# Pooled attention and a gated layer on one core: the denominators of 16 heads folded to 64 partitions, and the order searched

## The chip, the cores and the metric

The kernel runs on one core of a Trainium2 chip. The metric is the device time of one execution, in microseconds, as the median of several runs; less is better. Engine names are those of the profile: PE is the matrix engine (PEld its weight loads), DVE the vector engine, ACT the scalar engine, POOL the GpSimd engine, SP the queue that issues most transfers.

## What is computed

Attention with queries that are averaged in pairs, then a gated layer on its result. B = 4, H = 8, S = 1152, D = 64; d_model = 512, d_ff = 1536.

```python
q_pool = q.reshape(B, H, S // 2, 2, D).mean(axis=3)
scores = 1 / np.sqrt(D) * np.matmul(q_pool, k.transpose(0, 1, 3, 2))
scores = scores - np.max(scores, axis=-1, keepdims=True)
attn = np.exp(scores)
attn = attn / (np.sum(attn, axis=-1, keepdims=True) + 1e-09)
x = np.matmul(attn, v)          # then (B, H, S/2, D) -> (B * S/2, H * D)
gate = 1.0 / (1.0 + np.exp(-(x @ w_gate)))
out = (gate * (x @ w_val)) @ w_out
```

## The kernel before, in words

There are 32 heads, numbered u = 0 to 31, and each has 576 pooled queries in two halves of 288 columns (`GR`, `GN`). A half walks over 9 chunks of 128 keys (`NC`). To keep float32 accuracy, values are split into a high part in the type float32r and a low part that is what the high one left over, so that one product becomes two or three.

For one chunk of one half, `half` records: the scores, two products into a PSUM bank (L579); the exponential on ACT, once rounded to float32r into `eh` (L583) and once in full back into the bank (L612); the difference of the two on DVE into `el` (L615); the product of `eh` with the values into the bank `av[0]` (L622), and of `el` into `av[1]` (L626). Heads 0 to 7 (`WHOLE`) do it in plain float32 instead, with L597. Ahead of a head stand its maxima: 12 products of 384 columns (L473) and their reductions on DVE (L479).

The sum of the probabilities, the denominator, is built on POOL for heads 8 to 31. `acc` is [128, 2, 288]: POOL adds the `eh` tiles of two chunks at a time (L644), folds the two halves of `acc` into one (L651) and adds the ninth chunk (L654). Now every partition holds the sum over 9 keys, and what is left is a sum over 128 partitions. For that, ACT rounds `acc` to its high part (L692, `acc_hi`), POOL subtracts it to get the low part (L695, `acc_lo`), and PE multiplies each of the two [128, 288] tiles with a matrix of ones, `ones2`, into `av[1]` (L699, `den`). So the denominator takes two products for each half:

```python
for k in range(2):
    nc.tensor.matmul(out=tl(av[1])[:, 0:GN], lhsT=ones2, rhs=tl(dh)[:, k], start=False, stop=(k == 1))
```

After it DVE and ACT take the numerators and denominators out of the banks (L675 to L684), `normalise` divides, and splits the result into high and low parts `x` (L736, L740). The gated layer (`gated`, L815) of one batch element runs between the attention steps of the next one; the last one's runs alone at the end. Its operands `wg` and `wo` are loaded by SP, and its results pass DVE, ACT and POOL (L858, L864, L868, L872).

The order is not that of the code. `Plan` collects every step as an operation with an engine, an estimated duration, a priority and the buffers that it takes (`SLOTS` says how many there are of each: 4 `el`, 2 `t`, 2 `pp`, 1 `acc`, 2 `dh`, 8 banks `b`). `Plan.run` plays the plan through: each engine takes the ready operation with the lowest priority number, and the order that comes out is the order in which the instructions are emitted. Each engine then works through its own list in that order.

Of the kernel before, what the change touches and what calls it, by code (L numbers as in the profile page):

```python
# [37 lines left out]
class Plan:  # L38
# [16 lines left out]
    def op(self, eng, dur, fn, prio, after=(), uses=(), take=(), late=0.0, keep=0.0, behind=None):  # L55
# [7 lines left out]
        return o  # L63

    def run(self):
        n_dep = {}
        ready = {e: [] for e in self.LAT}
        for k, o in enumerate(self.ops):
            o.key = (o.prio, k)
            o.at = 0.0  # L70
            n_dep[o] = len(o.after)
            for a in o.after:
                a.users.append(o)
            if o.behind:
                n_dep[o] += 1
                o.behind.next.append(o)
# [3 lines left out]
        for t, hs in self.holds.items():  # L80
            for k, h in enumerate(hs):
                h.k = k
                left[h] = len(h.ops)
                for o in h.ops:
                    of.setdefault(o, []).append(h)
# [16 lines left out]
        while done < len(self.ops):  # L102
# [7 lines left out]
            while again:  # L110
                again = False
                for e in self.LAT:
# [34 lines left out]
                    for h in of.get(o, ()):  # L147
                        left[h] -= 1
                        h.end = max(getattr(h, "end", 0.0), av + o.keep)
                        if left[h] == 0:  # L150
                            free[h.tag].append((h.end, h.slot))
                            heapq.heappush(times, h.end)
# [10 lines left out]
def attention_glu_kernel(ctx: ExitStack, tc: tile.TileContext, qT, kT, vt_in, v, wg, wv, wo, out):  # L163
# [11 lines left out]
    SLOTS = {  # L175
# [20 lines left out]
    def tiles(tag, shape, dt, pool=const):  # L196
        n = LATE.get(tag, 0) or SECOND.get(tag, 0)
        return [None] * n + [pool.tile(shape, dt, name=f"{tag}{i}") for i in range(n, SLOTS[tag])]
# [8 lines left out]
    def change_first():  # L207
# [30 lines left out]
        "dh": tiles("dh", SHAPE["dh"], F32R),  # L238
        "t": tiles("t", SHAPE["t"], F32),
        "e": tiles("e", [128, GN], F32, first_p),  # L240
        "ve": tiles("ve", [128, NC, 2, D], F32, first_p),
# [27 lines left out]
    def pe64(n):  # L269
        return n / 595  # L270
# [12 lines left out]

    AHEAD = 50
    KEEP = 0.15
    LAST_GATE = 215
# [266 lines left out]
    def half(u, g, st, hd, stat, vdep, pair, tk):  # L553
# [13 lines left out]
        for c in range(NC):  # L567
# [22 lines left out]
            if whole:  # L590
# [8 lines left out]
                if c in RUNS:  # L599
                    last = pl.op("PE", 0.1 + len(wait) * pe64(GN), pv, pos + 1,  # L600
                                 after=deps + [vdep] + (in_turn if first else [last]),
                                 uses=[stat] + [h for _, h in wait] + ([] if first else av), take=av + tk if first else [])
                    if first:
                        in_turn[:] = [last]
                    wait, deps = [], []
# [82 lines left out]
        if mine_c:  # L688
# [7 lines left out]

            def den():
                for k in range(2):
                    nc.tensor.matmul(out=tl(av[1])[:, 0:GN], lhsT=ones2, rhs=tl(dh)[:, k], start=False, stop=(k == 1))  # L699

            o = pl.op("ACT", act(GN), acc_hi, at, after=added, uses=[acc], take=[dh])
            o = pl.op("POOL", 0.85, acc_lo, at, after=[o], uses=[acc, dh])
            last = pl.op("PE", 2 * pe(GN), den, at + 2, after=[o, last], uses=[dh, av[1]])
        st["yo"][g].append(pl.op("DVE", 0.46, plus2, at + 1, after=[part, last], uses=[av[1], y]))
# [251 lines left out]
    for k in range(SLOTS["Q"]):  # L956
        for t in TL["Q"][k]:
            nc.vector.memset(t[:, SQ:SQ + 64].bitcast(F32), 0.0)
    order = pl.run()
    with tc.manual_schedule():  # L960
# [36 lines left out]
```

## Time and profile before

| | |
|---|---|
| median of 3 runs | 922.13 us (921.84 to 923.32) |
| the profiled execution | 923.2 us, of which the span from first to last instruction is 921.4 us |
| instructions | 18477, of them 6299 matrix products |
| busy share | PE 98%, PEld 95%, POOL 73%, ACT 72%, DVE 70% |
| HBM | 169 GB/s over the span |
| granted clock of PE | 0.998 of full speed |

A busy share is a mean over stages that differ: up to about 160 us the heads in plain float32, the conversion of the weights and most transfers; then attention and gated layer together; from 801 us on the last gated layer alone. A product that is recorded with 295 ns overlaps the next one, so the distance between two starts, not the recorded length, tells what a product costs where nothing waits.

### The profile page before, as it was taken

Reading aid. Unit: us, or ns where it says so; the run is one execution under the profiler, and the core shown is the slowest. Engines: PE = TensorE matmul, PEld = TensorE weight load, DVE = VectorE, ACT = ScalarE, POOL = GpSimd, SP = SyncE. Lnnn points to the kernel's source line nnn. Section 1 sums busy time; section 2 is a strip of 40 time slices with the busy share of each in tenths; the row PEclk is TensorE's granted clock in tenths of the full one; section 3 lists DMA queues with packets and bytes.
Section 4 is the critical chain, followed back from the end, with each engine's and each line's share of the span. In section 5 each row is a group of like instructions: output and inputs, shape, how many; then the busy total and the mean of one; then the engine's idle time right before and its main releaser. Section 6 shows DMA issues by size and latency. Waiting matters only on the chain.

```text
span 921.4 us, 18477 instructions
## 1 busy us (share of the span) xinstructions
PE 904.3 (98%) x6299; PEld 873.9 (95%) x6299; DVE 649.4 (70%) x1428; ACT 659.9 (72%) x1703; POOL 672.3 (73%) x668
## 2 busy tenths in 40 slices
PE   6999999999999999999999999999999999999998
PEld 5888888999999999999999999999999999999998
DVE  7778768888899888778687878877677874510112
ACT  4888888989998787677887677677877777322111
POOL 6755455989889899788989889888989877521211
PEclk9999999999999999999999999999999999999999
DMA  6999888789958566555544455544545423435432
GB/s 149 232 278 260 268 263 245 227 274 272 292 181 274 177 212 194 157 156 162 152 123 144 141 156 158 165 134 140 161 126 158 142 92 116 164 140 179 164 115 75
DMA packets 57614, 166.25 MB, mean 180 GB/s; under 512 B 17392, under 2 KB 21744, under 8 KB 51376
## 3 DMA queue, kind: packets, MB, share of 16 engines
q1 hardware_dynamic: 57360, 164.78, 58.7%
q8 instruction: 49, 0.80, 0.4%
q14 instruction: 45, 0.37, 0.1%
q10 hardware_dynamic: 160, 0.30, 0.1%
HBM read 132.12 MB, written 23.59 MB: 169 GB/s over the span
## 4 chain that ended last, share of the span: by engine, by line
PE 93%; DVE 3%; ACT 2%; DMA 1%; issue 0%; POOL 0%; SPq 0%; ACTq 0%; DVEq 0%; POOLq 0%
PE bank L815 48%; PE bank L579 16%; PE bank L473 8%; PE bank L597 7%; PE bank L626 6%; PE bank L622 6%; PE bank L699 1%; DMA wo<-wo_d 1%; DMA qr<-in_qT_dram 0%; DVE pm L479 0%; DVE pm L386 0%; DVE el L615 0%; ACT e L583 0%; POOL acc L654 0%; DVE pp L479 0%
## 5 line engine op out<-in xcount | busy, mean ns | idle before, releaser
L815 PE MATMUL bank<-x,wg 128*128 128x288 f32 x2304 | 356.0, 295 | 0.1
L815 PEld LDWEIGHTS bank<-x,wg 128*128 128x128 f32 x2304 | 327.0, 188 | 0.9 <-DVE pm L479 0.5
L615 DVE TENSOR_TENSOR el<-bank,eh 128x288 fp32r<-128x288 f32 x432 | 192.8, 452 | 69.8 <-ACT bank L612 65.3
L479 DVE TENSOR_REDUCE pm<-bank 128x1 f32<-128x384 f32 (+1 forms) x375 | 200.5, 551 | 52.6 <-PE bank L473 49.0
L583 ACT ACTIVATE eh<-bank 128x288 fp32r<-128x288 f32 x432 | 176.9, 409 | 73.7 <-PE bank L579 64.8
L579 PE MATMUL bank<-QA,KA 128*128 128x288 f32 x576 | 177.6, 311 | 2.5 <-DVE el L615 1.2
L612 ACT ACTIVATE bank<-bank 128x288 f32<-128x288 f32 x432 | 176.8, 409 | 0.1
L579 PE MATMUL bank<-QB,KB 128*128 128x288 f32 x576 | 169.0, 296 | 1.7 <-DVE QB L305 1.7
L872 POOL TENSOR_TENSOR g<-sg,g 128x288 fp32r<-128x288 f32 x96 | 80.2, 835 | 108.6 <-ACT g L868 106.7
L644 POOL TENSOR_TENSOR acc<-acc,eh 128x576 f32<-128x576 f32 x92 | 132.8, 1444 | 17.3 <-ACT eh L583 15.4
L815 PE MATMUL bank<-g,wo 128*128 128x288 f32 x864 | 139.2, 296 | 1.1 <-DMA wo<-wo_d 0.9
L473 PE MATMUL bank<-KA,QA 128*128 128x384 f32 (+1 forms) x375 | 126.9, 347 | 1.4 <-ACT e L583 0.7
L626 PE MATMUL bank<-el,vt 128*128 128x288 f32 x432 | 127.5, 295 | 0.0
L622 PE MATMUL bank<-eh,vt 128*128 128x288 f32 x432 | 127.4, 295 | 0.0
L815 PEld LDWEIGHTS bank<-g,wo 128*128 128x128 f32 x864 | 124.7, 188 | 2.1 <-DMA wo<-wo_d 1.1
L579 PEld LDWEIGHTS bank<-QA,KA 128*128 128x128 f32 x576 | 108.9, 189 | 9.0 <-DVE el L615 2.0
L579 PEld LDWEIGHTS bank<-QB,KB 128*128 128x128 f32 x576 | 109.1, 189 | 3.3 <-POOL qr L424 1.9
L864 DVE SCALAR_TENSOR_TENSOR sg<-sg,bank 128x288 f32<-128x288 f32 x96 | 43.2, 450 | 79.8 <-PE bank L815 77.9
L626 PEld LDWEIGHTS bank<-el,vt 128*128 128x128 f32 x432 | 81.1, 188 | 0.7 <-DVE y L678 0.3
L622 PEld LDWEIGHTS bank<-eh,vt 128*128 128x128 f32 x432 | 81.0, 188 | 0.5 <-ACT eh L583 0.2
L858 ACT ACTIVATE sg<-bank 128x288 f32<-128x288 f32 x96 | 39.4, 411 | 56.2 <-PE bank L815 54.0
L644 POOL TENSOR_TENSOR acc<-eh,eh 128x576 f32<-128x576 f32 x48 | 68.7, 1431 | 13.9 <-ACT eh L583 9.7
(83 smaller groups left out, 1380.4 us busy)
## 6 DMA issues: line engine op xcount, KB each, us to landing
wg<-wg_d SPq DMA_DIRECT2D x48, 1024.0 KB, 5.1
wo<-wo_d SPq DMA_DIRECT2D x36, 512.0 KB, 3.8
kr<-in_kT_dram SPq DMA_DIRECT2D x62, 288.0 KB, 5.2
wg_d<-cs SPq DMA_DIRECT2D x24, 512.0 KB, 5.3
qr<-in_qT_dram SPq DMA_DIRECT2D x31, 288.0 KB, 4.0
KP<-KA SPq DMA_DIRECT2D x30, 288.0 KB, 3.8
vr<-in_v_dram SPq DMA_DIRECT2D x24, 288.0 KB, 3.4
cr<-in_wg_dram SPq DMA_DIRECT2D x12, 512.0 KB, 5.9
```

What stands on the lines that cost most here:

```text
L473: nc.tensor.matmul(out=tl(m)[LO if t == 4 else ALL, 0:384], lhsT=lhs(t), rhs=rhs()[:, j * 384:(j + 1) * 384], start=True, stop=True)
L479: nc.vector.tensor_reduce(out=o, in_=tl(m)[p, 0:384], axis=AXX, op=ALU.max)
L579: nc.tensor.matmul(out=tl(m)[:, 0:GN], lhsT=tl(hd["k"])[k][:, ks], rhs=tl(hd["q"])[k][:, a:b], start=(k == 0), stop=(k == 1))
L583: nc.scalar.activation(out=ev(), in_=tl(m)[:, 0:GN], func=ACTF.Exp, scale=1.0 / 16.0)
L597: nc.tensor.matmul(out=tl(av[0])[:, 0:GN], lhsT=pair(c, 0), rhs=tl(h), start=(c == 0), stop=(c == NC - 1))
L612: nc.scalar.activation(out=p, in_=p, func=ACTF.Exp, scale=1.0 / 16.0)
L615: nc.vector.tensor_tensor(out=tl(el), in0=tl(m)[:, 0:GN], in1=ev().bitcast(F32), op=ALU.subtract)
L622: nc.tensor.matmul(out=tl(av[0])[:, 0:GN], lhsT=pair(c, w), rhs=ev(), start=(c == 0), stop=(c == NC - 1))
L626: nc.tensor.matmul(out=tl(av[1])[:, 0:GN], lhsT=pair(c, 1 - w), rhs=tl(el), start=(c == 0), stop=(c == NC - 1 and not mine_c))
L644: nc.gpsimd.tensor_tensor(out=tl(acc), in0=tl(old).bitcast(F32), in1=tl(eh).bitcast(F32), op=ALU.add)
L815: nc.tensor.matmul(out=ps[:, 0:GN], lhsT=l, rhs=r, start=(n == 0 and j == 0), stop=(n == 3 and j == 2))
L872: nc.gpsimd.tensor_tensor(out=g[:, 1, a:b], in0=tl(sg), in1=g[:, 0, a:b].bitcast(F32), op=ALU.subtract)
```

## The change

For heads 16 to 31 (`FOLD`) the sum over partitions is begun before PE. ACT copies the upper 64 partitions of `acc` into a new tile `ft` on partitions 0 to 63 (`down`, L745 of the changed kernel), and POOL adds it to the lower 64 (`fold2`, L749). The high part of this [64, 288] sum is written to the lower half of `dh[:, 0]` (`half_hi`, L736) and its low part to the upper half of the same tile (`half_lo`, L739), so that one product with ones over 128 partitions sums both (`den`, L730).

To make room, `el` has 3 buffers instead of 4, `t` and `pp` 1 instead of 2. The planner's estimate of the plain float32 product step (L597) loses its constant 0.1. And the order is taken from `search`: 30 times it draws a stretch of 30 us of the plan, shifts the priority of every operation in it (but those of SP) by up to 1 either way, plans anew, and keeps the shifts if the plan does not end later.

```diff
+    def search(self, rounds, width, shift):
+        dice = random.Random(1)
+        best = self.run()
+        end = max(o.end for o in best)
...
+        for _ in range(rounds):
+            at = dice.uniform(-width, end)
+            near = [(o, o.prio) for o, s, _ in made if at <= s <= at + width and o.eng != "SP"]
+            for o, p in near:
+                o.prio = p + dice.uniform(-shift, shift)
+            order = self.run()
+            new = max(o.end for o in order)
+            if new <= end:
+                best, end = order, new
...
+            else:
+                for o, p in near:
+                    o.prio = p
...
-        "b": 8, "K": 3, "Q": 3, "kr": 1, "qr": 1, "vr": 1, "vt0": 1, "vt1": 1, "eh": 4, "el": 4, "acc": 1, "dh": 2,
-        "t": 2, "pm": 2, "pp": 2, "KP": 1, "e": 6, "ve": 2,
+        "b": 8, "K": 3, "Q": 3, "kr": 1, "qr": 1, "vr": 1, "vt0": 1, "vt1": 1, "eh": 4, "el": 3, "acc": 1, "dh": 2, "ft": 1,
+        "t": 1, "pm": 2, "pp": 1, "KP": 1, "e": 6, "ve": 2,
...
+        "ft": tiles("ft", [64, GN], F32),
...
+    FOLD = lambda u: u >= 16
...
-                    last = pl.op("PE", 0.1 + len(wait) * pe64(GN), pv, pos + 1,
+                    last = pl.op("PE", len(wait) * pe64(GN), pv, pos + 1,
...
             def den():
+                if FOLD(u):
+                    nc.tensor.matmul(out=tl(av[1])[:, 0:GN], lhsT=ones2, rhs=tl(dh)[:, 0], start=False, stop=True)
+                    return
                 for k in range(2):
                     nc.tensor.matmul(out=tl(av[1])[:, 0:GN], lhsT=ones2, rhs=tl(dh)[:, k], start=False, stop=(k == 1))
 
+            def half_hi():
+                nc.scalar.activation(out=tl(dh)[LO, 0], in_=tl(acc)[LO, 0], func=ACTF.Copy)
+
+            def half_lo():
+                nc.gpsimd.tensor_tensor(out=tl(dh)[HI, 0], in0=tl(acc)[LO, 0], in1=tl(dh)[LO, 0].bitcast(F32), op=ALU.subtract)
+
+            if FOLD(u):
+                ft = pl.hold("ft")
+
+                def down():
+                    nc.scalar.activation(out=tl(ft), in_=tl(acc)[HI, 0], func=ACTF.Copy)
+
+                def fold2():
+                    o = tl(acc)[LO, 0]
+                    nc.gpsimd.tensor_tensor(out=o, in0=o, in1=tl(ft), op=ALU.add)
+
+                o = pl.op("ACT", 0.43, down, at, after=added, uses=[acc], take=[ft])
+                added = [pl.op("POOL", 0.85, fold2, at, after=[o], uses=[acc, ft])]
+                acc_hi, acc_lo = half_hi, half_lo
             o = pl.op("ACT", act(GN), acc_hi, at, after=added, uses=[acc], take=[dh])
             o = pl.op("POOL", 0.85, acc_lo, at, after=[o], uses=[acc, dh])
-            last = pl.op("PE", 2 * pe(GN), den, at + 2, after=[o, last], uses=[dh, av[1]])
+            last = pl.op("PE", (2 - FOLD(u)) * pe(GN), den, at + 2, after=[o, last], uses=[dh, av[1]])
...
-    order = pl.run()
+    order = pl.search(30, 30.0, 1.0)
```

On POOL, at the end of the first half of head 21, before: the ninth chunk's addition (L654), and the subtraction that makes the low part (L695).

```order
L424 TENSOR_TENSOR qr_87<-qr_87 64x576
L644 TENSOR_TENSOR acc_99<-acc_99,eh_92 128x576
L651 TENSOR_TENSOR acc_99<-acc_99 128x288
L654 TENSOR_TENSOR acc_99<-acc_99,eh_93 128x288
L695 TENSOR_TENSOR dh_100<-acc_99,dh_100 128x288
L305 TENSOR_TENSOR QB_84<-ident,pm_112 64x4x64 x2
```

Nothing stands between L654 and L695 on POOL; ACT's rounding (L692) falls between the two in time. In the changed kernel POOL has at the same place (L685 is the ninth chunk's addition, L749 `fold2`, L739 the subtraction):

```order
L682 TENSOR_TENSOR acc_98<-acc_98 128x288
L685 TENSOR_TENSOR acc_98<-acc_98,eh_93 128x288
L336 TENSOR_TENSOR QB_84<-ident,pm_111 64x4x64 x2
L749 TENSOR_TENSOR acc_98<-acc_98,ft_102 64x288
L572 TENSOR_TENSOR vt_89<-vr_88,vt_89 128x9x64
L739 TENSOR_TENSOR dh_99<-acc_98,dh_99 64x288
L455 TENSOR_TENSOR qr_87<-qr_87 64x576
```

One more addition on POOL, and two operations of other steps (L336, the diagonals for a later head; L572, the low part of its values) have moved into the two gaps in which ACT copies and rounds.

On PE, up to the denominator of the same half, before: the ninth chunk's two products (L622 and L626 with `eh_93`, `el_97`), then the next half's first chunks, pieces of the gated layer (L815), and the denominator (L699).

```order
L622 MATMUL bank<-eh_93,vt_90 128x288
L626 MATMUL bank<-el_97,vt_90 128x288
L815 MATMUL bank<-g_1446,wo_135 128x288 x3
L622 MATMUL bank<-eh_91,vt_90 128x288
L579 MATMUL bank<-QA_80,KA_74 128x288
L579 MATMUL bank<-QB_83,KB_77 128x288
L626 MATMUL bank<-el_98,vt_90 128x288
L815 MATMUL bank<-g_1447,wo_135 128x288 x3
L815 MATMUL bank<-g_1448,wo_135 128x288 x3
L815 MATMUL bank<-g_1449,wo_135 128x288 x3
L699 MATMUL bank<-dh_100,sel 128x288 x2
```

In the changed kernel the last rows ahead of it are these (L653 and L657 are the products with `eh` and `el`, L610 the scores, L868 the gated layer, L730 the denominator):

```order
L657 MATMUL bank<-el_97,vt_90 128x288
L868 MATMUL bank<-g_1436,wo_134 128x288 x3
L653 MATMUL bank<-eh_92,vt_90 128x288
L610 MATMUL bank<-QA_80,KA_74 128x288
L610 MATMUL bank<-QB_83,KB_77 128x288
L657 MATMUL bank<-el_96,vt_90 128x288
L868 MATMUL bank<-g_1437,wo_134 128x288 x3
L730 MATMUL bank<-dh_99,sel 128x288
```

There is one product with `dh` instead of two, and it stands later: between the ninth chunk's product with `el` and the denominator there were 16 products before, and there are 50 now.

## Rows read from the trace of the kernel before

**Rows 1.** The page's head and busy times (share of the span).

```profile
span 921.4 us, 18477 instructions
...
PE 904.3 (98%) x6299; PEld 873.9 (95%) x6299; DVE 649.4 (70%) x1428; ACT 659.9 (72%) x1703; POOL 672.3 (73%) x668
```

**Rows 2.** The page's chain that ended last, by engine and by line.

```profile
PE 93%; DVE 3%; ACT 2%; DMA 1%; issue 0%; POOL 0%; SPq 0%; ACTq 0%; DVEq 0%; POOLq 0%
PE bank L815 48%; PE bank L579 16%; PE bank L473 8%; PE bank L597 7%; PE bank L626 6%; PE bank L622 6%; PE bank L699 1%; DMA wo<-wo_d 1%; DMA qr<-in_qT_dram 0%; DVE pm L479 0%; DVE pm L386 0%; DVE el L615 0%; ACT e L583 0%; POOL acc L654 0%; DVE pp L479 0%
```

**Rows 3.** Stretches of the span: busy us and instructions of each engine, clock, DMA.

```profile
core 0: us, PE busy (x) PEld busy (x) DVE busy (x) ACT busy (x) POOL busy (x), PEclk, DMA share, GB/s
0.00:160.00 160.00, 148.57 (x763) 126.26 (x764) 122.06 (x260) 129.10 (x310) 93.50 (x100) 0.99 0.86 243
160.00:376.00 216.00, 214.94 (x1550) 210.41 (x1549) 187.81 (x413) 188.46 (x488) 194.24 (x190) 1.00 0.75 234
376.00:801.00 425.00, 423.63 (x3108) 420.36 (x3107) 320.40 (x715) 318.05 (x850) 364.36 (x355) 1.00 0.47 144
801.00:921.40 120.40, 117.12 (x882) 116.89 (x882) 19.15 (x42) 24.29 (x57) 20.25 (x26) 1.00 0.39 132
```

**Rows 4.** Waits over the span: us, times, longest us.

```profile
PE bank L381 <- DVE QA L347: 6.7, 1, 6.7
...
PEld bank L815 <- DMA wo<-wo_d: 1.1, 1, 1.1
```

**Rows 5.** Line L699 in 376 to 801: ns min/median/max, first and last start.

```profile
L699 PE MATMUL bank<-dh,sel x64: 290/295/403, 382.8 to 797.6; 128*128 128x288 f32 x64
its engine sat idle before it (us, times) until:
  POOL dh L695: 0.5, 2
```

**Rows 6.** The chain that ended last from 801 us on: start us, us, what.

```profile
801.11 117.14 PE bank L815 x882
```

**Rows 7.** POOL's lines in 376 to 801: busy us, mean ns, idle before.

```profile
L644 POOL TENSOR_TENSOR acc<-acc,eh 128x576 f32<-128x576 f32 x63 | 91.1, 1447 | 11.7 <-ACT eh L583 10.8
...
L651 POOL TENSOR_TENSOR acc<-acc 128x288 f32<-128x288 f32 x32 | 28.4, 887 | 2.4
L654 POOL TENSOR_TENSOR acc<-acc,eh 128x288 f32<-128x288 f32 x32 | 28.1, 878 | 2.0
L695 POOL TENSOR_TENSOR dh<-acc,dh 128x288 fp32r<-128x288 f32 x32 | 26.6, 833 | 6.0 <-ACT dh L692 5.0
...
L450 POOL TENSOR_TENSOR KB<-kr,KA 64x576 fp32r<-64x576 f32 x13 | 20.3, 1561 | 1.6 <-ACT KA L444 0.8
```

**Rows 8.** Stretch 320 to 360, columns as in rows 3.

```profile
320.00:360.00 40.00, 40.00 (x298) 39.88 (x297) 31.91 (x68) 31.44 (x85) 38.31 (x39) 1.00 0.69 216
```

**Rows 9.** ACT's lines in 376 to 801, columns as in rows 7.

```profile
L583 ACT ACTIVATE eh<-bank 128x288 fp32r<-128x288 f32 x280 | 114.4, 408 | 55.4 <-PE bank L579 49.6 <-DVE y L678 1.1 <-issue 0.5
...
L692 ACT ACTIVATE dh<-acc 128x288 fp32r<-128x288 f32 x32 | 14.1, 441 | 5.2 <-POOL acc L654 5.1
...
L675 ACT ACTIVATE t<-bank 64x288 f32<-64x288 f32 x32 | 13.0, 406 | 3.7 <-PE bank L622 2.6
```

**Rows 10.** Waits in 376 to 801, columns as in rows 4.

```profile
POOL g L872 <- ACT g L868: 18.3, 27, 1.7
POOL acc L644 <- ACT eh L583: 18.0, 23, 1.8
...
POOL dh L695 <- ACT dh L692: 5.0, 8, 1.0
```

**Rows 11.** DVE's lines in 376 to 801, columns as in rows 7.

```profile
L615 DVE TENSOR_TENSOR el<-bank,eh 128x288 fp32r<-128x288 f32 x281 | 125.5, 453 | 58.5 <-ACT bank L612 55.5
...
L450 DVE TENSOR_TENSOR KB<-kr,KA 64x576 fp32r<-64x576 f32 x14 | 13.9, 993 | 0.4
...
L434 DVE TENSOR_TENSOR QA<-qr,QA 64x576 fp32r<-64x576 f32 x13 | 10.5, 807 | 0.6
```

**Rows 12.** Order of time around 504 us: start us, us, engine, instruction.

```profile
504.13 0.86 DVE L434 TENSOR_TENSOR QA<-qr,QA 64x576 fp32r<-64x576 f32 x1
...
504.46 1.21 POOL L695 TENSOR_TENSOR dh<-acc,dh 128x288 fp32r<-128x288 f32 x1
```

More of the change, by code (lines that the diff above doesn't have):

```diff
@@ L1 @@
 import heapq
+import random
 from contextlib import ExitStack
@@ L63, in op @@
         return o
+    def search(self, rounds, width, shift):
+        dice = random.Random(1)
+        best = self.run()
+        end = max(o.end for o in best)
+        made = [(o, o.start, o.end) for o in best]
+        slots = [(h, h.slot) for hs in self.holds.values() for h in hs]
+        for _ in range(rounds):
[7 more added lines that the diff above has]
+                best, end = order, new
+                made = [(o, o.start, o.end) for o in best]
+                slots = [(h, h.slot) for hs in self.holds.values() for h in hs]
+            else:
+                for o, p in near:
+                    o.prio = p
+        for o, a, b in made:
+            o.start, o.end = a, b
+        for h, s in slots:
+            h.slot = s
+        return best
     def run(self):
@@ L67, in run @@
         ready = {e: [] for e in self.LAT}
+        for o in self.ops:
+            o.users, o.next = [], []
         for k, o in enumerate(self.ops):
@@ L81, in run @@
             for k, h in enumerate(hs):
-                h.k = k
+                h.k, h.end = k, 0.0
                 left[h] = len(h.ops)
@@ L148, in run @@
                         left[h] -= 1
-                        h.end = max(getattr(h, "end", 0.0), av + o.keep)
+                        h.end = max(h.end, av + o.keep)
                         if left[h] == 0:
```

## The prediction, made before the run

> **What bounds the kernel now.** I read the page's head and its busy times first. TensorE is busy for 904.3 of the span's 921.4 us, its weight loads, which overlap the products, for 873.9, and no other engine passes 73% [rows 1]. The profiled execution took 923.2 us, 1.8 us more than its span and 1.07 us more than the median of the runs, 922.13; the sum below is made against 923.2 and the 1.07 is taken off at the end. Next I read the chain that ended last: 93% of it is PE, in all the product lines, and the line that the change thins out, L699, is in it with 1% [rows 2]. A mean over the kernel does not say whether a saved product is worth its length where it stands, so the third view is the table of stretches [rows 3]. The 32 denominator steps of heads 16 to 31 run from 382.8 to 797.6 us [rows 5], so the stretch 376 to 801 is theirs: PE is busy there for 423.63 of 425 us, at a granted clock of 1.00, while POOL has 364.36, DVE 320.40 and ACT 318.05. PE's own idle time in that stretch is 1.37 us, 1.1 of it one wait for a weight load near the end [rows 4]. TensorE bounds this stretch by itself, and what is taken from it there comes off the end, as long as nobody else becomes late.
>
> **The change part by part.**
>
> *Products removed.* In L699 two products with ones become one, in 16 heads x 2 halves = 32 places; the order of the changed kernel has the single rows (PE pieces above). All have 288 columns. A product's own record says 290 to 403 ns [rows 5], but products overlap, so that is not its price. The price is the distance from one to the next where nothing waits: 882 products of 288 columns in 117.14 us, 132.8 ns each [rows 6]. In the stretch itself it is 423.63 us / 3108 = 136.3 ns [rows 3], which holds 191 longer products of 384 columns. I take 132.8: 32 x 0.1328 = **4.25 us**; the other end is 32 x 0.1363 = 4.36. The weight load of each removed product goes with it.
>
> *POOL work added.* 32 times `fold2`, 288 columns on 64 partitions. Half the partitions are not cheaper on POOL: 64x576 takes 1561 ns, 128x576 1447 [rows 7]. The nearest rows are the other POOL operations of 288 columns in this stretch, 833 to 887 ns [rows 7]; I take L651's 887, the same operation on the same tile: 32 x 0.887 = 28.4 us (low end 26.7). The subtraction that makes the low part stays one instruction. POOL then has 364.4 + 28.4 = 392.8 us of work in a stretch that PE needs for 425 - 4.25 = 420.75: 93%. I cost it at nothing, and PE is the cover. That POOL can be so full without PE waiting is in the trace: from 320 to 360 us it was busy for 38.31 of 40 us (96%) and PE for 40.00 [rows 8].
>
> *ACT work added.* 32 copies `down`, 64x288 from SBUF. 64-partition copies cost what 128-partition ones do (L675 406 ns, L583 408), and the nearest row, L692's copy of the same tile, has 441 ns [rows 9]: 32 x 0.441 = 14.1 us, on an engine with 107 us idle in the stretch [rows 3]. Nothing on the path.
>
> *A longer chain to the denominator.* After the last addition to `acc` the way to PE was ACT, POOL, PE; it becomes ACT, POOL, ACT, POOL, PE. The addition is 0.441 + 0.887 us and two hand-overs; POOL's recorded waits for ACT at this place are 5.0 us in 8 cases, 0.6 each [rows 10], so about 1.3 + 1.2 = 2.5 us. On PE the order answers this: between the last score product of a half and its denominator stand 38 to 56 products before (median 45, 6.0 us at 132.8 ns) and 48 to 94 after (median 67, 8.9 us). The median grows by 2.9 us, the chain by 2.5. The only waits of PE for this chain in the trace of before are two, 0.5 us together [rows 5]. On POOL, which takes its instructions in order, a round trip to ACT costs a wait only where no other operation stands in the gap. Before, 7 of the 32 gaps are empty; in the new order 5 of 64 are (the POOL pieces show a filled half). At 0.6 us each that is 3 us of waits against 4.2 before, off PE's path. I cost it at nothing. If a denominator is late all the same, the bank it closes is freed later, the next half's score products wait for a bank, and PE idles.
>
> *What lies behind POOL's subtraction.* It frees the only `acc` buffer; the next half's first addition takes it, and that one frees two `eh` buffers for the exponentials. That is the queue behind a late `fold2`. It is the mechanism of the last rival.
>
> *Smaller buffers* (`el` 4 to 3, `t` 2 to 1, `pp` 2 to 1). `t` is written once a half, 425 / 32 = 13.3 us apart, `pp` once a pair. For `el`, DVE's subtraction takes 453 ns [rows 11], and in the new order at least 13 products (1.7 us) stand between the product that frees a buffer and the one that needs it filled again. Nothing.
>
> *The search over the order.* It moves rows on every engine in the whole kernel, and the number of instructions outside the fold is the same. What it can win is PE's idle time that is not fixed: 11.43 us in 0 to 160, less the 6.7 us until the first operands are there, 1.06 in 160 to 376, 1.37 in the fold's stretch [rows 3, 4]: 7.2 us. What it can lose has no row; I bound it by the same amount. I take zero, with half of it, 3.6 us, to either side: before 160 us the new order is nearly the old one with neighbours exchanged, and the first gated product is the 613th in both. The SP queue's last weight load, for which PE waits, stands in the same place.
>
> *One rule against the change.* The trace shows POOL slowed by DVE: while DVE ran L434 (0.86 us, two SBUF inputs) the POOL subtraction that began inside it took 1.21 us where its mean is 0.833 [rows 7, 12]. With 13.9 + 10.5 us of such DVE work in the stretch [rows 11] and 32 new POOL operations, 27 DVE operations x 32 x (0.887 + 0.90) / 425 = 3.6 meetings of about 0.4 us: 1.4 us on POOL or DVE, neither of them the bound. The Trainium skill (SBUF — State Buffer, "Who interferes with whom") goes further: a DVE instruction with two SBUF inputs and a GpSimd one that reads SBUF exclude each other, and the loser waits for the whole instruction. By the row the sum keeps its 4.25; by the rule, with every meeting ending on PE's path, it would be an estimated 4.25 - 1.4 = 2.85, or 919.3. That is inside the third case below.
>
> **Sum.** 923.2 - 4.25 = 918.95 for an execution like the profiled one, and 922.13 - 4.25 = **917.9 us** at the median. A measurement of this kernel can tell about 0.2% (1.85 us) from no change, so faster means below 920.3.
>
> **The ways it could go.**
> 1. *Forecast, 70%*: 917.9, its own range 916 to 920.
> 2. *The search also closes gaps, 8%.* For it: 7.2 us of idle that is not fixed. Against it: these are many small gaps in a part where every engine is busy. Half of it: 917.9 - 3.6 = 914.3.
> 3. *The gain is eaten on the way, 15%.* Late denominators, an `el` that waits, meetings of DVE and POOL, or a worse order early on, up to 3.6 us: 921.5, within 0.2% of before. For it: from 380 us on PE has nearly no idle, so any wait is a new one. Against it: the cover counted above.
> 4. *POOL becomes the bound, 7%, slower.* In 376 to 801 POOL has 60.6 us of idle now, most of it waits in its queue (36 us for ACT's `g` and exponentials [rows 10]). The added work takes it to 392.8 us, so POOL decides as soon as more than 420.75 - 392.8 = 28 us of waits are left, and the kernel is slower than before from 425 - 392.8 = 32 us on, 53% of today's. With three quarters left, 45.5 us, the stretch is 438.3 us and the kernel 922.13 + 13.3 = 935.4. Against it: the 96% of [rows 8], the fewer empty gaps, and that a queue that is fuller waits less.
> That the products are not removed is excluded by the order: 32 single rows.
>
> **How the numbers follow.** Faster by over 0.2%: cases 1 and 2, 0.78. Within 0.2%: case 3, 0.15. Slower: case 4, 0.07. The range runs from 914.6, between the forecast and the whole gain of the search, to 921.8, past case 3: it leaves out case 4, a part of case 2 and the edge of case 3.
>
> **What would show it.** Right: in the profile after, L730 (the denominator) has 64 products, 32 fewer; PE's span shrinks by about 4 us with its idle time unchanged; in the stretch of heads 16 to 31 POOL is at 92 to 95%, PE still above 99%; the new POOL line (L749) takes 0.81 to 0.89 us and the new ACT line (L745) 0.44. Wrong: PE's waits name POOL's `dh`, ACT's exponentials or DVE's `el` with more than 2 us in that stretch (case 3); PE falls below 97% there with POOL near 100% (case 4); or PE's idle before 376 us shrinks by over 2 us (case 2).

## The result, and the profile after

The changed kernel takes 930.04 us (median of 4 runs, 928.31 to 931.61) against 922.39 for the kernel before beside it: ratio 1.0076 [1.0064, 1.0088], 0.76% slower. The prediction said 917.9 and "faster".

The page's head, busy times and chain of the changed kernel; before: [rows 1, 2].

```profile
span 929.8 us, 18536 instructions
...
PE 908.4 (98%) x6267; PEld 872.3 (94%) x6267; DVE 655.8 (71%) x1428; ACT 672.7 (72%) x1735; POOL 696.5 (75%) x700
...
PE 77%; ACT 7%; DVE 6%; POOL 4%; issue 2%; DMA 2%; SPq 0%; ACTq 0%; POOLq 0%; DVEq 0%
```

The 32 products are gone (6299 to 6267), and yet the span grew by 8.4 us. The chain that ended last was 93% PE and is 77% PE: ACT, DVE and POOL now have shares in it. The stretches, columns as in [rows 3]:

```profile
0.00:160.00 160.00, 149.28 (x770) 127.33 (x771) 123.48 (x258) 128.36 (x308) 94.81 (x101) 0.99 0.84 236
160.00:376.00 216.00, 213.56 (x1525) 207.13 (x1524) 189.43 (x407) 188.90 (x485) 189.19 (x185) 1.00 0.75 233
376.00:801.00 425.00, 419.90 (x3031) 412.48 (x3030) 318.76 (x711) 327.81 (x877) 385.76 (x384) 1.00 0.46 141
801.00:929.80 128.80, 125.68 (x948) 125.41 (x946) 24.12 (x54) 27.63 (x66) 26.73 (x33) 1.00 0.41 140
```

In 376 to 801 us PE ran 77 products fewer than before in the same 425 us, 31 of them removed ones; the others, and some from the stretch ahead, were pushed past 801, where 66 more run than before. PE idles for 5.1 us there instead of 1.37. POOL has 386 us of work, 91%, not 100%. Waits over the span, columns as in [rows 4]:

```profile
PE bank L412 <- DVE QA L378: 6.8, 1, 6.8
PEld bank L657 <- DVE el L646: 5.4, 12, 1.1
PEld bank L868 <- DMA wo<-wo_d: 3.1, 1, 3.1
PEld bank L730 <- POOL dh L739: 2.9, 8, 0.7
PE bank L657 <- DVE el L646: 2.6, 7, 0.8
```

The first row was there before (6.7). The product with `el`, one load of `wo`, and the denominator now wait. Idle time undercounts this, because a recorded product covers the start of the next one. So I also add up, over all successive products, the distance between their starts beyond the 131.5, 172 and 243 ns that one of 288 columns, of 384, and of the plain float32 kind takes where nothing waits. This sum of **lost time** is 33.3 us before and 45.9 after: 12.6 more, and 12.6 - 4.25 us of removed products is the 8.4 us of span. Largest additions between 160 and 800 us, by what the product waited for: `el` 1.0 to 5.8, the `wo` load 0 to 3.0, `dh` 0.4 to 2.7, and short gaps for which the trace names no releaser, 5.8 to 10.3.

The new and changed lines in 376 to 801, columns as in [rows 7]:

```profile
L749 POOL TENSOR_TENSOR acc<-acc,ft 64x288 f32<-64x288 f32 x31 | 25.3, 815 | 7.3 <-ACT ft L745 6.5
L739 POOL TENSOR_TENSOR dh<-acc,dh 64x288 fp32r<-64x288 f32 x31 | 25.2, 813 | 3.6 <-ACT dh L736 0.6 <-POOL x L793 0.5 <-POOL g L925 0.4
...
L745 ACT ACTIVATE ft<-acc 64x288 f32<-64x288 f32 x31 | 13.7, 443 | 6.8 <-POOL acc L685 6.2
```

Prices as forecast (0.815 for 0.887, 0.443 for 0.441), and 6.5 us of POOL's waits are for the new copy. The one `wo` load, in order of time (start us, us, queue or engine, what):

```profile
436.72 0.49 SPq L442 DMA_DIRECT2D qr<-in_qT_dram  x1
437.26 0.58 SPq L884 DMA_DIRECT2D wo<-wo_d  x1
...
437.88 1.36 SPq L439 DMA_DIRECT2D kr<-in_kT_dram  x2
...
445.07 0.67 PE L868 MATMUL bank<-g,wo 128*128 128x288 f32 x3 [2.85 <-DMA wo<-wo_d]
```

It was issued between a load of `qr` and two of `kr`, and PE got it 7.8 us after its issue. In the kernel before this load was issued at 434.9 us, 2.4 us earlier, and landed after 4.6. The median landing of such a load in the changed kernel is 3.9 us:

```profile
wo<-wo_d SPq DMA_DIRECT2D x36, 512.0 KB, 3.9
```

### The profile page after: what moved, and what is told of

Same layout as the page of the kernel before. It is cut to its first block, busy times and chain, and to the rows that moved or that the text cites. A ratio compares the mean times of both kernels' runs of the same rounds, so it can differ in the third digit from the quotient of the medians.

```text
span 929.8 us, 18536 instructions
## 1 busy us (share of the span) xinstructions
PE 908.4 (98%) x6267; PEld 872.3 (94%) x6267; DVE 655.8 (71%) x1428; ACT 672.7 (72%) x1735; POOL 696.5 (75%) x700
## 4 chain that ended last, share of the span: by engine, by line
PE 77%; ACT 7%; DVE 6%; POOL 4%; issue 2%; DMA 2%; SPq 0%; ACTq 0%; POOLq 0%; DVEq 0%
PE bank L868 39%; PE bank L610 13%; PE bank L628 7%; PE bank L504 6%; PE bank L657 5%; PE bank L653 5%; ACT eh L614 2%; ACT bank L643 1%; DVE el L646 1%; DVE pm L510 1%; DMA kr<-in_kT_dram 1%; DVE QA L465 1%; DMA wo<-wo_d 1%; POOL acc L675 1%; PE bank L730 1%
## 5 line engine op out<-in xcount | busy, mean ns | idle before, releaser
L868 PE MATMUL bank<-x,wg 128*128 128x288 f32 x2304 | 354.1, 295 | 0.0
L868 PEld LDWEIGHTS bank<-x,wg 128*128 128x128 f32 x2304 | 325.6, 188 | 1.5 <-DVE el L646 0.6
L610 PE MATMUL bank<-QA,KA 128*128 128x288 f32 x576 | 176.8, 311 | 2.3 <-ACT e L614 1.1
L610 PE MATMUL bank<-QB,KB 128*128 128x288 f32 x576 | 167.9, 296 | 1.7 <-DVE QB L336 1.7
L925 POOL TENSOR_TENSOR g<-sg,g 128x288 fp32r<-128x288 f32 x96 | 79.6, 829 | 98.8 <-ACT g L921 97.3
L868 PE MATMUL bank<-g,wo 128*128 128x288 f32 x864 | 140.9, 297 | 2.9 <-DMA wo<-wo_d 2.9
L675 POOL TENSOR_TENSOR acc<-acc,eh 128x576 f32<-128x576 f32 x92 | 135.9, 1477 | 9.8 <-ACT eh L614 5.6
L657 PE MATMUL bank<-el,vt 128*128 128x288 f32 x432 | 129.5, 301 | 2.7 <-DVE el L646 2.6
L868 PEld LDWEIGHTS bank<-g,wo 128*128 128x128 f32 x864 | 125.7, 189 | 3.7 <-DMA wo<-wo_d 3.1
L653 PE MATMUL bank<-eh,vt 128*128 128x288 f32 x432 | 128.3, 297 | 0.3
L610 PEld LDWEIGHTS bank<-QA,KA 128*128 128x128 f32 x576 | 108.8, 189 | 9.7 <-ACT e L614 2.3
L610 PEld LDWEIGHTS bank<-QB,KB 128*128 128x128 f32 x576 | 108.7, 189 | 3.3 <-POOL qr L455 1.9
L657 PEld LDWEIGHTS bank<-el,vt 128*128 128x128 f32 x432 | 81.2, 188 | 6.7 <-DVE el L646 5.4
L653 PEld LDWEIGHTS bank<-eh,vt 128*128 128x128 f32 x432 | 81.3, 188 | 2.2 <-ACT eh L614 1.4
L628 PE MATMUL bank<-e,ve 128*128 128x288 f32 x288 | 78.2, 412 | 0.0
```

The costliest lines, as they stand in the source:

```text
L610: nc.tensor.matmul(out=tl(m)[:, 0:GN], lhsT=tl(hd["k"])[k][:, ks], rhs=tl(hd["q"])[k][:, a:b], start=(k == 0), stop=(k == 1))
L628: nc.tensor.matmul(out=tl(av[0])[:, 0:GN], lhsT=pair(c, 0), rhs=tl(h), start=(c == 0), stop=(c == NC - 1))
L653: nc.tensor.matmul(out=tl(av[0])[:, 0:GN], lhsT=pair(c, w), rhs=ev(), start=(c == 0), stop=(c == NC - 1))
L657: nc.tensor.matmul(out=tl(av[1])[:, 0:GN], lhsT=pair(c, 1 - w), rhs=tl(el), start=(c == 0), stop=(c == NC - 1 and not mine_c))
L675: nc.gpsimd.tensor_tensor(out=tl(acc), in0=tl(old).bitcast(F32), in1=tl(eh).bitcast(F32), op=ALU.add)
L868: nc.tensor.matmul(out=ps[:, 0:GN], lhsT=l, rhs=r, start=(n == 0 and j == 0), stop=(n == 3 and j == 2))
```

## The experiments

Theory at the start: the longer chain to the denominator eats more than the product is worth. Rivals: the order that the search found; POOL's load; the smaller buffers. Every ratio is against the kernel before on the same chip. Only the kernels of runs 3 and 12 contain the search. The planner plans each edit anew, so every one also shuffles the order, and the intervals do not include what that may do. For unfolded kernels with the short chain it is little: runs 3, 4, 6, 13 and 18 moved the order and stayed within 0.1%. For folded ones it is much: the change and runs 1, 2, 10 and 12 lie anywhere from 0.20 to 0.76%. So a difference of a few tenths of a per cent between two folded kernels may be the order's.

### Taking the change apart

**1. The change without its search.**

```diff
-    order = pl.search(30, 30.0, 1.0)
+    order = pl.run()
```

> The changed kernel with the planner's plain order (no search); fold, smaller buffers and the new estimate for the plain float32 step stay. Theory S (the searched order brings the new waits): 918 to 921 us, near the forecast, and PE's waits for el and for the wo load are as before. Theory F (the fold, with its longer chain and fuller POOL, eats more than it saves): 927 to 931 us. Theory E (three el buffers): 926 to 930 us, with PE waiting for el as in the changed kernel (2.6 us by the waits view).

927.53 us, 1.0041 [1.0027, 1.0055].

**2. The fold alone**: run 1 with `"el": 4` and the old estimate of L597.

```diff
-                    last = pl.op("PE", len(wait) * pe64(GN), pv, pos + 1,
+                    last = pl.op("PE", 0.1 + len(wait) * pe64(GN), pv, pos + 1,
```

> The kernel before with the fold alone: el keeps 4 buffers (t and pp have 1, which makes room for ft), no search, old estimate. Theories S and E: 917.5 to 920 us (32 products of 132.8 ns less). Theory F: 925 us or more, with the waits of PE for POOL's dh at over 2 us.

926.31 us, 1.0032 [1.0021, 1.0043].

**3. The search alone**, on the kernel before with its buffers and two products.

```diff
-    FOLD = lambda u: u >= 16
+    FOLD = lambda u: False
```

> The kernel before with the search alone (30 rounds, same seed), no fold, buffers and estimate as before. Theory S: 926 to 934 us, slower than before by 4 us or more. Theories F and E: 920 to 924 us, no change.

924.45 us, 1.0008 [0.9999, 1.0017].

**4. The smaller buffers alone**, in the kernel before.

```diff
-"el": 4, ... "t": 2, "pm": 2, "pp": 2
+"el": 3, ... "t": 1, "pm": 2, "pp": 1
```

> The kernel before with el 3, t 1, pp 1 and nothing else. Theory E: 925 to 929 us, and PE waits for el over 2 us. Theories S and F: 921 to 924 us.

923.69 us, 0.9997 [0.9988, 1.0007]. The fold by itself is 0.32% slower; small buffers are free here; the search by itself costs nothing that can be told, and on top of the fold it costs 0.35% more (1.0041 to 1.0076).

**12. Another seed in the changed kernel.**

```diff
-        dice = random.Random(1)
+        dice = random.Random(2)
```

> The changed kernel with another seed of the search (2 for 1), all else as in the change. Theory S2 (the searched orders lose the same wherever the dice fall): 1.006 to 1.010, as with seed 1 (1.0076). Theory L (one unlucky order, above all its 3 us wait for a wo load): 1.000 to 1.005.

925.24 us, 1.002 [1.0009, 1.0032], 0.56% below seed 1, and its one wait of PE for a `wo` load is 0.7 us, where seed 1 has 3.1 and run 1 0.8. So the search's part is a draw: -0.2% with one seed, +0.35% with the other, against run 1.

### Each price by itself

**5. The products alone.** Heads 16 to 31 of the kernel before multiply only the high part with ones; the low part is made as before but left out of the denominators, so the chain is unchanged.

```diff
+                n = 1 if u >= 16 else 2
-                for k in range(2):
+                for k in range(n):
```

> The kernel before, with one of the two denominator products left out in heads 16 to 31; the low part of those denominators is still made and not used (this part of the result is left out), and nothing is added. It prices the 32 products. If they are worth what they take on PE (the prediction's first term): 4.25 us less than before, ratio 0.9954. Theory O (a new order costs about what the products give, whatever is changed): 0.998 to 1.002.

919.01 us, 0.9948 [0.9933, 0.9963]: 4.2 us of 923.2 (0.52%), the 4.25 forecast.

**6. POOL's load alone.** 32 operations on a scratch tile behind the ninth addition, which nobody waits for (`t` and `pp` have one buffer, as in the fold).

```diff
+                def extra():
+                    nc.gpsimd.tensor_tensor(out=tl(ft), in0=tl(ft), in1=tl(ft), op=ALU.subtract)
+                pl.op("POOL", 0.85, extra, at, after=added, take=[ft])
```

> The kernel before with both products, and one POOL operation of 64x288 more in each half of heads 16 to 31, on a scratch tile that nobody reads: fold2's load without its place in the chain and without the saving. Theory P (POOL's fuller queue makes the others late): slower by 5 us or more, ratio 1.005 to 1.008. Theory C (the longer chain to the denominator): 0.999 to 1.002.

923.14 us, 0.9998 [0.9989, 1.0007]. The stretch, columns as before:

```profile
376.00:801.00 425.00, 424.37 (x3115) 421.45 (x3113) 324.30 (x717) 318.90 (x853) 381.92 (x389) 1.00 0.48 144
```

The scratch operation on POOL, columns as in [rows 7]:

```profile
L706 POOL TENSOR_TENSOR ft<-ft 64x288 f32<-64x288 f32 x32 | 21.7, 678 | 0.0
```

It adds 21.7 us to POOL, where `fold2` adds 25.3, and PE is as busy as before. POOL's load by itself is not it.

**9. The chain alone.** Two products as before, but a copy on ACT and an addition on POOL stand between the ninth addition and the rounding; their result is unused (`t` and `pp` again have one buffer).

```diff
+                o = pl.op("ACT", 0.43, down, at, after=added, uses=[acc], take=[ft])
+                added = [pl.op("POOL", 0.85, extra, at, after=[o], uses=[acc, ft])]
```

> The kernel before with both products, and the chain to the denominator made longer by an ACT copy and a POOL addition whose result nobody reads (the rounding to the high part waits for them): the fold's chain without its saving. Theory C (the longer chain costs): about 7 us slower, the 2.95 us of the fold alone plus the 4.25 us that it saves, ratio 1.006 to 1.009. If instead the single product or the fold's own tiles matter: 0.999 to 1.002.

927.66 us, 1.0046 [1.003, 1.0063]. The waits of PE's weight loads in 376 to 801:

```profile
PEld bank L627 <- DVE el L616: 3.0, 5, 1.0
...
PEld bank L700 <- POOL dh L696: 0.9, 2, 0.6
```

32 POOL operations that were free beside the chain in run 6 cost 0.46% as links of it, together with the copy on ACT: more than any new order of an unfolded kernel did. But it lies between the two ranges, and it is not the whole loss of the fold, which is 0.32% slower and gives away the 0.52% of run 5: 0.84% together. The other 0.38% stand in no run by themselves.

Most of the waits it brings are not for the denominator but for `el`. Two of the five at L627, 1.8 of 3.0 us, come close behind an operation of DVE with both inputs in SBUF (L451) that took 1.49 and 2.12 us; ten of the 27 such operations in the changed kernel take 0.75 us. The second (start us, us, engine, what):

```profile
559.54 1.43 POOL L425 TENSOR_TENSOR qr<-qr 64x576 f32<-64x576 f32 x1
...
560.24 2.12 DVE L451 TENSOR_TENSOR KB<-kr,KA 64x576 fp32r<-64x576 f32 x1
560.93 0.81 POOL L884 TENSOR_TENSOR g<-sg,g 128x288 fp32r<-128x288 f32 x1
561.70 1.31 POOL L709 TENSOR_TENSOR ft<-ft,acc 64x288 f32<-64x288 f32 x1
562.39 0.82 DVE L616 TENSOR_TENSOR el<-bank,eh 128x288 fp32r<-128x288 f32 x2
...
562.90 0.40 PE L627 MATMUL bank<-el,vt 128*128 128x288 f32 x1 [0.62 <-DVE el L616]
```

L709, the added operation, is held up in its turn: 1.31 us for 0.80. So some of these waits come of DVE and POOL holding each other up; the last section has the size.

### Relieving one engine

**7. `fold2` on DVE** instead of POOL, in run 2.

```diff
-                    nc.gpsimd.tensor_tensor(out=o, in0=o, in1=tl(ft), op=ALU.add)
+                    nc.vector.tensor_tensor(out=o, in0=o, in1=tl(ft), op=ALU.add)
```

> The fold alone (four el, no search), with its addition fold2 on DVE instead of POOL: the same steps in the chain, 26 us less on POOL, 15 us more on DVE. Theory P: 0.995 to 0.997, the whole 4.25 us or nearly. Theory C: 1.001 to 1.004, as with fold2 on POOL (1.0032).

930.86 us, 1.0077 [1.006, 1.0094]: slower than both ranges.

**8. One of the normalising products moved from POOL to DVE** for half the pairs, in run 2.

```diff
-    NMP = lambda p: True
+    NMP = lambda p: p < 8
```

> The fold alone with fold2 on POOL, and POOL relieved elsewhere: the normalising product of heads 16 to 31 (16 operations of 0.81 us) goes to DVE. The chain to the denominator is untouched. Theory P: about half of the loss comes back, 0.998 to 1.001. Theory C: 1.002 to 1.004.

933.22 us, 1.0104 [1.0088, 1.012], slower than both ranges too. The stretch of 7 and of 8, in two fences, then the first wait of PE in 8:

```profile
376.00:801.00 425.00, 420.25 (x3029) 411.28 (x3029) 337.45 (x740) 330.30 (x879) 361.37 (x353) 1.00 0.46 139
```

```profile
376.00:801.00 425.00, 415.75 (x3018) 409.04 (x3017) 332.90 (x723) 329.66 (x878) 372.57 (x367) 1.00 0.46 139
```

```profile
PEld bank L657 <- DVE el L646: 7.4, 7, 2.0
```

POOL has less to do (361 and 373 us, 387 in run 2) and the kernel is slower. But neither run is a clean relief of POOL, for both put operations with two inputs in SBUF on DVE, and there they wait for POOL. In run 8 the moved product (L775) takes 0.46 us where nothing meets it and 1.01 in the mean, and each of the seven waits at L657 ends within 2 us of the start of one:

```profile
415.12 1.43 POOL L675 TENSOR_TENSOR acc<-eh,eh 128x576 f32<-128x576 f32 x1
415.51 1.34 DVE L775 TENSOR_TENSOR y<-y,r 128x288 f32<-128x288 f32 x1
...
416.89 0.46 DVE L646 TENSOR_TENSOR el<-bank,eh 128x288 fp32r<-128x288 f32 x1
...
417.40 0.40 PE L657 MATMUL bank<-el,vt 128*128 128x288 f32 x1 [0.88 <-DVE el L646]
```

In run 7 it is the denominator that is late: PE's weight loads wait 4.9 us for `dh` (2.2 in run 2) and 1.2 for `el`.

### What the late chain holds

**10. The denominator planned later**, in run 2.

```diff
-... den, at + 2, after=[o, last], ...
+... den, at + 4, after=[o, last], ...
```

> The fold alone, with the denominator's priority two chunks later in the plan (at + 4 for at + 2). Theory C1 (PE arrives at the denominator before its operand): PE's waits for POOL's dh fall under 0.5 us and the time to 0.996 to 0.999. Theory C2 (what is held longer costs: the single acc, the bank): no better than the fold alone, 1.003 to 1.006.

926.35 us, 1.0026 [1.0017, 1.0035], a little below the second range. The order changed, but the product still stands right behind the low part, 0.2 us after it in the median: the edit gave no slack, and tells nothing of what slack is worth.

**11. `acc` freed early**: the folding addition L682 writes a tile `ac` of its own (`el` 3 to make room), so that the next half can start on `acc`; in run 2.

```diff
-... out=tl(acc)[:, 0], in0=tl(acc)[:, 0], in1=tl(acc)[:, 1], op=ALU.add)
+... out=tl(ac) if ac else tl(acc)[:, 0], in0=tl(acc)[:, 0], in1=tl(acc)[:, 1], op=ALU.add)
```

> The fold alone, with a tile of its own (ac, [128, 288]) for the folded sum, so that acc is free for the next half as soon as its two halves are added, before the whole chain (el has 3 buffers to make room). Theory C2 (the single acc, held through the longer chain, delays POOL's first addition of the next half, the eh buffers and the exponentials): 0.995 to 0.998. Theory C1: 1.002 to 1.005.

925.85 us, 1.002 [1.001, 1.0029].

**13. The bank held longer, without a longer chain**, in the kernel before.

```diff
-... 2 * pe(GN), den, at + 2, ...
+... 2 * pe(GN), den, at + (5 if u >= 16 else 2), ...
```

> The kernel before, unfolded, with the denominator's priority in heads 16 to 31 three chunks later (at + 5): the bank av[1] is held as long as in the fold (18.5 us of products in the median, 15.1 before), while chain, POOL and products stay. Theory B (the bank held longer is what costs): 1.003 to 1.006. Theories A and Z (acc, or no slack at the denominator): 0.999 to 1.002.

922.42 us, 0.9994 [0.9985, 1.0003]. Here the denominator stands 3.6 us behind its low part, and nothing is lost.

**14. A PSUM bank of its own for the denominator**, in run 2, so that `av[1]` is read without waiting for it.

```diff
+                sums = pl.hold("b")
...
-... out=tl(av[1])[:, 0:GN], lhsT=ones2, rhs=tl(dh)[:, 0], start=False, stop=True)
+... out=tl(sums)[:, 0:GN], lhsT=ones2, rhs=tl(dh)[:, 0], start=True, stop=True)
```

> The fold alone, with a PSUM bank of its own for the denominator, taken when its product is due: av[1] is free when the last low product is in, chain or not. Theory B: 0.995 to 0.998. Theories A and Z: 1.001 to 1.004, as the fold alone (1.0032).

922.52 us, 0.9998 [0.9988, 1.0007], between the two ranges.

**15. Own bank and own `ac`**: the edits of 14 and 11 together.

> As the one before, and acc freed early (the tile ac, el with 3 buffers): neither the bank nor acc is held through the chain. Theories A and B: 0.995 to 0.997. Theory Z: 0.999 to 1.002, with PE's waits for POOL's dh still at 2 us or more.

922.15 us, 0.9989 [0.9979, 0.9998], again between them; PE's weight loads wait 0.9 us for `dh`.

**16. The same, and the plan is told that the low part comes 0.8 us later than it does**, which moves the denominator back.

```diff
-            o = pl.op("POOL", 0.85, acc_lo, at, after=[o], uses=[ac or acc, dh])
+            o = pl.op("POOL", 0.85, acc_lo, at, after=[o], uses=[ac or acc, dh], late=0.8 * FOLD(u))
```

> As the one before, and the planner is told that the low part comes 0.8 us later than POOL's time, so that the denominator stands later in PE's list. Theory Z: 0.995 to 0.997, PE's waits for POOL's dh under 0.5 us. If none of the three is it: 1.000 or more.

919.55 us, 0.996 [0.9945, 0.9975]: faster than both kernels.

**17. Only the 0.8 us** (the edit of 16), in run 2, with the shared bank and `acc`.

> The fold alone, without the search, with only the plan told that the low part arrives 0.8 us later than it does (no bank and no acc tile of its own). If the missing slack in front of the denominator is the whole loss of the fold, this gains nearly what the run with all three mends did: 919.5 to 920.5. If the bank and acc that a late denominator holds are needed as well, it stays between: 922 to 925. If the run with all three mends was a lucky order, it is near the fold alone, 926.

930.14 us, 1.0078 [1.0064, 1.0092]: all three guesses missed.

**18. Only the 0.8 us, in the kernel before** (the edit of 16 with `late=0.8 * (u >= 16)`, two products).

> The kernel before, two products, no fold, with the same 0.8 us of slack told to the plan for heads 16 to 31. It has 0.3 us of slack and next to no waits for the denominator, so slack has nothing to win: 922 to 924 where the mended fold's gain is the products'. A gain of over 2 us here would mean that the mended fold owes its time to the slack or to the order, and not to the products.

922.08 us, 0.9991 [0.9982, 1.0]. So in the kernel before slack is worth some 0.09%, by the interval at most 0.18%. Between runs 15 and 16, with the fold, it is 0.29%; how much of that is the slack and how much the order that came with it is not shown.

The stretch of run 16, then what is left there of PE's waits for `el` (no wait for `dh` is left):

```profile
376.00:801.00 425.00, 423.65 (x3113) 421.30 (x3113) 327.98 (x721) 331.22 (x887) 388.80 (x391) 1.00 0.47 145
```

```profile
PEld bank L660 <- DVE el L649: 1.2, 2, 1.0
```

And waits in run 17, where the denominator is never late either:

```profile
ACT r L715 <- PE bank L730: 15.9, 17, 1.8
...
PEld bank L657 <- DVE el L646: 7.6, 14, 1.1
```

With POOL at 388.80 us, among the fullest of all, run 16 has PE at 423.65 of 425, as before the change. In run 17 the wait only changed its place: the product with `el` waits 7.6 us instead of the denominator. ACT stands 15.9 us before its copy of the denominator (7.3 before the change, 9.7 in run 13, which loses nothing); that this wait makes `el` late is a guess.

The runs side by side. Slack is the median time from the end of POOL's low part to the start of its product with ones, over the 32 places; the waits are those of PE's weight loads in 376 to 801 us, added up over PE's lines (a dash: none listed); lost time as above, over the span of the profiled execution (in run 14 that one took 1.6 us more than the median).

| run | slack us | for `dh` us | for `el` us | lost us | ratio |
|---|---|---|---|---|---|
| before | 0.3 | 0.5 | - | 33.3 | 1 |
| after | 0.2 | 2.9 | 2.5 | 45.9 | 1.0076 |
| 2, fold alone | 0.3 | 2.2 | 2.7 | 40.6 | 1.0032 |
| 9, chain alone | 0.2 | 0.9 | 3.0 | 36.8 | 1.0046 |
| 13, bank held | 3.6 | - | - | 33.4 | 0.9994 |
| 14, own bank | 0.2 | 2.3 | 1.3 | 38.4 | 0.9998 |
| 15, own bank and `ac` | 0.3 | 0.9 | 1.7 | 36.0 | 0.9989 |
| 17, slack alone | 1.1 | - | 8.8 | 44.5 | 1.0078 |
| 16, all mends | 1.0 | - | 1.2 | 33.9 | 0.996 |

## Why the prediction was wrong

**The step that failed** is "A longer chain to the denominator", costed at nothing because the products in front of the denominator grew by 2.9 us where the chain grew by 2.5. The size of the chain was right: from the end of the ninth addition to the denominator it is 2.6 us in the median before and 4.9 in run 2. What was wrong was to call the products between a cover. They are the planner's answer to the chain: it places the product with ones where it expects the low part, no later. From the last score product to the end of the low part it is 5.9 us in the median before and 9.2 after; to the denominator 6.2 and 9.3. The distance grew as the chain did and the slack stayed at 0.2 to 0.3 us. The chain also scatters more now: its longest case lies 2.0 us above its median before, 2.9 after. The cover should have been counted against the actual end of the low part, in the trace of before: it would have read 0.3 us, too little for a chain with two more hand-overs. Run 9 prices the longer chain at 0.46% [0.30, 0.63], about what the products give.

By the runs the 0.76% add up so: 0.52% gained by the products (5); 0.46% lost by the chain (9), 0.38% by the fold beyond that (2 against 5 and 9), 0.09% by the smaller buffers and the new estimate on top of the fold (1 against 2, inside the noise), and 0.35% by the search (the change against 1). What the 0.38% are, something of the fold or its order, stays open.

**What was behind it** was named in "What lies behind POOL's subtraction", but not priced. The next chunks' `el` comes late, that is in the rows. That it does so because a late chain holds `acc`, the bank or ACT's queue is argued, and the runs decide little of it. Freeing `acc` alone (11) is 0.12% better than the fold's 0.32%, slack alone (17) worse; an own bank is 0.34% better (14), and all three together bring most of the gain back (16). The differences between 2, 11 and 17 are of the size that a new order makes, and only 14, 15 and 16 lie below every folded kernel without an own bank. That the held bank by itself is the cause is refuted by 13: holding it longer is free as long as the chain is short. In 14 the denominators are as late as in run 2 (2.3 us of waits, 0.2 of slack) and only the waits for `el` are halved. Why an own bank helps so much, and how much of its gain is the order that was planned with it, stays open.

**The meetings of DVE and POOL** were put at 1.4 us for the new operations, off the path. On POOL that is nearly the size: of the 62 operations of L749 and L739 in the stretch two took 1.20 and 1.21 us, 0.4 more than the 0.8 of the others, and one 0.89, together 0.9 us. One of them in order of time (start us, us, engine, what):

```profile
398.05 1.02 DVE L481 TENSOR_TENSOR KB<-kr,KA 64x576 fp32r<-64x576 f32 x1
398.52 1.21 POOL L749 TENSOR_TENSOR acc<-acc,ft 64x288 f32<-64x288 f32 x1
```

`fold2` began 0.47 us into DVE's operation and took 0.4 us longer, somewhat less than the 0.55 that DVE still had to go. The Trainium skill (SBUF — State Buffer, "Who interferes with whom") lets the loser wait until the other instruction is done; this row agrees with that to 0.15 us. On DVE it was too small. Its 27 operations with two inputs in SBUF took 13.9 + 10.5 = 24.4 us before [rows 11], meetings included, and 29.9 after:

```profile
L465 DVE TENSOR_TENSOR QA<-qr,QA 64x576 fp32r<-64x576 f32 x14 | 16.5, 1176 | 0.4
L481 DVE TENSOR_TENSOR KB<-kr,KA 64x576 fp32r<-64x576 f32 x13 | 13.4, 1029 | 0.5 <-ACT KA L475 0.2
```

That sum is not a price: it is 28.8 us in run 6 and 30.2 in run 13, which lose nothing. A meeting costs where an `el` that PE needs soon stands behind it, as in runs 8 and 9, and so it is in the changed kernel: in five of the seven waits of PE's weight loads for `el` in the stretch, 1.8 of 2.5 us, the late `el` directly follows an L465 or L481 that took 1.2 to 1.8 us. That the meetings lie off the path is refuted by these rows. No run takes them out, so how much of the fold's loss is theirs, beyond these 1.8 us, is not known.

**The search** was taken at zero with 3.6 us to either side. It was a draw of that size: 0.35% of 923 us is 3.2 us against run 1 with seed 1, and 1.9 us in favour with seed 2. Of seed 1's loss, 3.0 us stand at one `wo` load. The prediction considered only the last weight load; it was one at 437 us that came late. The search shifts no priority of SP's, so SP's order must have moved through the buffers that its loads wait for; that was argued, not tried.

**Right:** the price of a product (run 5: 4.2 us for 4.25); POOL's added time (25.3 us for 28.4, free as mere load in run 6) and ACT's (13.7 for 14.1); the smaller buffers (run 4). A small misreading changes nothing: the 1.1 us of [rows 4] is the wait of the weight load, and it ends at 801.1 us; of PE's 1.37 us of idle time it is 0.75.

**The rivals.** The third had the mechanism, late denominators and an `el` that waits, but capped it at 3.6 us and forgot that the search's loss can come on top; by the sum of lost time the whole change lost 12.6. The fourth had the sign and not the cause: POOL never became the bound (91% in the stretch; runs 6 and 16). The sign that I gave for it, PE below 97% with POOL near 100%, did not come: PE has 98.8%. The third's did, over 2 us of waits for `dh` and for `el`.

## What to carry to other kernels

Products that stand between a chain and its consumer are cover only beyond the moment at which the chain ends: read from the trace how long before the consumer's start its operand was ready, and price a longer chain against that number. Work that is free as load on a busy engine (run 6) can cost 0.4% as a link in a chain (run 9), and the waits then show at what stands behind the chain more than at its own end. Work moved from POOL to DVE is not out of POOL's way while both its inputs lie in SBUF (runs 7 and 8).

What brings a saved product back is less sure. Of the folded kernels only those with a bank of their own for the denominator ended level or faster, and the one with slack besides kept most of the gain (16); slack alone did not help (17). Each of them is one order of the plan, and orders of the fold alone differ by half a per cent: several should be measured before a single part is given the credit.

## What the runs showed of the hardware

Operations of DVE and POOL with two inputs in SBUF hold each other up, and the size can be read from `fold2` on DVE. Run 7, columns as in [rows 7], then the same line as in [rows 5]:

```profile
L749 DVE TENSOR_TENSOR acc<-acc,ft 64x288 f32<-64x288 f32 x31 | 21.7, 698 | 2.6 <-ACT ft L745 2.0
```

```profile
L749 DVE TENSOR_TENSOR acc<-acc,ft x31: 440/487/1557, 382.3 to 792.5; 64x288 f32<-64x288 f32 x31
```

The mean of 698 ns is no price. Undisturbed it is 440, much as DVE's subtraction of 288 columns with one operand in a PSUM bank (453 [rows 11]); POOL's `fold2` has a median of 799. The long ones began inside an operation of POOL, here with 0.87 us of it to go (start us, us, engine, what):

```profile
463.32 1.43 POOL L455 TENSOR_TENSOR qr<-qr 64x576 f32<-64x576 f32 x1
...
463.88 1.18 DVE L749 TENSOR_TENSOR acc<-acc,ft 64x288 f32<-64x288 f32 x1
```

It took 1.18 us: 0.44 and the 0.87 less 0.13. All 31 fit that to 0.02 us: their own 0.44, and what is left of the POOL operation that runs when they begin, less 0.13. The same fits, with their own undisturbed times, the 15 moved products of run 8 and in the changed kernel the 27 operations of L465 and L481; and the other way round, the 62 of L749 and L739 on POOL against the operations of DVE with two inputs in SBUF. Who begins first pays nothing. A second operation of POOL that follows at once can still get in first: L451 in run 9 waited for L425 and L884, and its 2.12 us are 0.75 and the 1.50 until L884 ended, less 0.13.

On POOL the addition of two tiles of 64x288 takes 0.80 us and the subtraction of a tile from itself 0.66 (medians, the change and run 6). A load of `wo` issued between a load of `qr` and two of `kr` landed after 7.8 us in the changed kernel, for a median of 3.9. Two loads of the kernel before with the same neighbours (at 452.5 and 669.0 us) took 5.7 and 5.1, so the neighbours are not all of it.
